# Weight splits moved from GpSimd to VectorE, and the last stage's weight conversion spread over more steps

## The chip, the cores and the metric

The kernel runs on one core of a Trainium2 chip. The metric is device time in microseconds for one execution, the median of three runs. The engines of the core are named as in the profile: PE is TensorE's matmul queue, PEld its weight loads, DVE is VectorE, ACT is ScalarE, POOL is GpSimd, SP is SyncE, which here issues most DMAs.

## The reference

The inputs are float32 except the last stage's two weights, which arrive as float64. Three stages follow one another on 2304 tokens of 512 values:

```
x   = local_attention(q, k, v) + upsampled(pooled_attention(q, k, v))   # 4 batches, 8 heads
e   = argmax(x @ w_gate + modality_bias[modality_id])                   # 8 experts
y   = prob[e] * (relu(x @ w1[e]) @ w2[e])                               # w1[e] 512x1024, w2[e] 1024x512
h   = y @ w_in                                                          # 512 -> 2048
out = (max(h, 0) + log1p(exp(-abs(h)))) @ w_out                         # 2048 -> 512
```

One pass of the array is less exact than the result is wanted. So every operand a of a matmul is kept as two float32r tensors, high = round(a) and low = a - high, and each product is three matmuls: high x high, low x high, high x low (lines L553, L556 and L557 of a helper).

## The kernel before, in words

**The attention and the gate** take the first 220 us or so. The gate computes the expert's logits of a group of tokens and turns them into a choice, a probability and a rank by some twenty small VectorE operations on tiles of 128 x 40 (L862 to L895 are the first), each of which needs the one before. For the last group, TensorE can go on only when these are done.

**The experts** work on slots of 128 rows. A slot gathers its rows (L522, an indirect DMA that GpSimd issues), multiplies by the expert's w1 (`gemm1`), applies relu (`h_t`), multiplies by w2 (`gemm2`), scales the result on ScalarE (L1171, `y`) and stores it. Two slots, 9 and 15, hold the remains of two experts each and are called mixed; 20 slots run for this input. Operands are split into high and low as well: `split_t` does so for the rows, with the subtraction on VectorE at L528 (`xl` for the input rows, `hl` for the hidden ones).

**The weights** come in parts of 128 x 1024 float32; a slot with an expert's weights of its own needs eight. A part is loaded to a buffer `raw`, and `split_part` makes of it `wh` (ScalarE copies and rounds, L332) and `wl` (raw minus wh, L333). Which engine does L333 is decided by the part's number i: for the first full slots' run (i < bounds[0]) GpSimd does it for every fourth part and for parts 4 to 7; for the last stage's parts c = 8 to 15 (i >= FF0 + CD) GpSimd does it always; VectorE does the others. That makes 45 of 152 splits on GpSimd. The subtraction needs `wh`, so it stands behind L332 of the same part.

**The conversion** turns the last stage's float64 weights into float32 by integer operations on halves of a part: SP loads a half (`conv_load`), and `conv_work` issues four operations, on ScalarE (L206, `cm`), VectorE (L209, `cy`, then L213) and GpSimd (L215, which adds `cm`). For the first eight parts (c < CD) this is done during the slots from 7 on as the code is written, and the result is stored to memory and loaded again like other weights. For parts 8 to 15 it is done within the last stage, straight into a `raw` buffer, and `split_part` follows.

**The last stage** has 18 tiles of 128 tokens in 6 groups of three, and 16 parts c of 128 hidden columns. A step is one group and one part: `ffn1` multiplies by the w_in part and applies the function with four or five VectorE operations (L1238, L1240, L1241, L1246; L1237 only from group 2 on), and two steps later `ffn2` multiplies by the w_out part. The list `steps` sets the order. Before, it goes (group 0, c 0 to 7), (group 1, c 0 to 7), (group 0, c 8 to 15), (group 1, c 8 to 15), then each later group with all 16 parts. `acts` hangs further work on the steps: the conversion of half i = 0 to 15 at step i + 2, the split of part 8 + i//2 in the same step as its second half, the gathers of a later group's rows (L1193, issued by GpSimd) and their transposes (`y_t`, with a small cast of an index column on VectorE, L1215, that needs the gather).

**What sets the order.** Each engine runs its own instruction queue in order, and an instruction that waits holds up all behind it. The order in a queue is chosen by a scheduler that simulates the program when it is built; instructions marked with `keep_in_program_order` keep the order in which they are written. So a change of one assignment can move other instructions too.

The choice of the engine for the subtraction, L332 to L334:

```
ins = (act.activation(out=hi, in_=r, func=ACTF.Copy),
       (pool if i >= FF0 + CD or (i % 4 == 3 or NR[0] <= i < PL) and i < bounds[0] else dve).tensor_tensor(
           out=lo, in0=r, in1=f32(hi), op=ALU.subtract))
```

Of the kernel before, what the change touches and what calls it, by code (L numbers as in the profile page):

```python
# [19 lines left out]
def tile_attention_moe_ffn(  # L20
# [30 lines left out]
    # Slots of 128 rows. A full one holds a block of one expert: the first NSTAT the first blocks of the expert with the most  # L51
    # rows before the last group, the others the further blocks of more than 64 rows. A mixed one (in MIX) holds two experts'
    # last 64 rows or fewer. Slots from SM on are for the draws that need them.
# [209 lines left out]
    def load_part(i):  # L263
        """Starts the load of a part, if the part before it in its tile is split."""
        kind, s, j = parts[i]
        at = raw_of(kind, s, j)
        if at not in raws or owner.get(at, i) not in split and at in owner:
            return False
        owner[at] = i
        t = raws[at]  # L270
        if kind == 3:
            x = sp.dma_start(out=t, in_=wf[s])
            if NR[0] <= s < 8:
                tc.keep_in_program_order(x)
        else:
            w = w1r if kind == 1 else w2r
            if s < NSTAT:
                if "star" not in eids:
                    eids["star"] = sp.value_load(star_i[0:1, 0:1], min_val=0, max_val=NE - 1)
                sp.dma_start(out=t, in_=w[bass.ds(eids["star"] * DM + j * 128, 128), :])  # L280
            else:
                if s not in eids:
                    eids[s] = sp.value_load(widx[0:1, dix[s]:dix[s] + 1], min_val=0, max_val=2 * NE - 1)
                e = eids[s]
                r = (e & (NE - 1)) * DM + j * 128
                if s >= SM:
                    sp.dma_start(out=t, in_=w[bass.ds(r, 128), :])
                else:
                    with tc.If(e < NE):
                        sp.dma_start(out=t, in_=w[bass.ds(r, 128), :])  # L290
        loaded.add(i)
        return True

    def ring_of(i):
        """0, 1: the two pools of the ring; 2: the further parts that the feed-forward holds."""
        if i < bounds[0]:
            return 0 if i % NRT < NR[0] else 1
        c = i - FF0
        return 0 if c < 0 or NRT - NR[0] <= c < NRT else 1 if c < NRT else 2

    def load_mixed(i):
        """The parts of two experts, not split."""
        kind, s, j = parts[i]
        at = ring_of(i)
        w = w1r if kind == 1 else w2r
        ts = []
        for a, nm in enumerate(("wh", "wl")):
            t = ring[at].tile([128, 1024], F32, tag=nm, name=nm, bufs=NR[at])
            d = NDF + 2 * MIX.index(s) + a
            if (s, a) not in eids:  # L310
                eids[s, a] = sp.value_load(widx[0:1, d:d + 1], min_val=0, max_val=NE - 1)
            sp.dma_start(out=t, in_=w[bass.ds(eids[s, a] * DM + j * 128, 128), :])
            ts.append(t)
        split[i] = ts

    def split_part(i):
        for n in range(i, min(i + 8, state["end"], FF0 + CD)):
            if parts[n][1] in MIX and parts[n][0] < 3:
                continue
            if n not in loaded and not load_part(n):  # L320
                break
        if parts[i][1] in MIX and parts[i][0] < 3:
            return load_mixed(i)
        at = ring_of(i)
        if at < 2:
            hi = ring[at].tile([128, 1024], F32R, tag="wh", name="wh", bufs=NR[at])
            lo = ring[at].tile([128, 1024], F32R, tag="wl", name="wl", bufs=NR[at])
        else:
            hi, lo = extra.pop(0)
        assert i in loaded or i >= FF0 + CD  # L330
        r = raws[raw_of(*parts[i])]
        ins = (act.activation(out=hi, in_=r, func=ACTF.Copy),  # L332
               (pool if i >= FF0 + CD or (i % 4 == 3 or NR[0] <= i < PL) and i < bounds[0] else dve).tensor_tensor(  # L333
                   out=lo, in0=r, in1=f32(hi), op=ALU.subtract))  # L334
        if PL <= i < PIN or i < NR[0]:
            tc.keep_in_program_order(ins[1])
            tc.keep_in_program_order(ins[0])
        if i >= FF0:
            for x in ins:
                tc.keep_in_program_order(x)  # L340
        split[i] = (hi, lo)

    def part(kind, s, j):
        """A part's two tensors; splits a few of those that follow, too."""
        i = where[kind, s, j]
        n = 2
        for k in range(i, min(i + state["ahead"] + 1, state["end"])):
            if k not in split and (k == i or n):
                split_part(k)
                n -= k > i  # L350
        return split[i]

    # ================= slot tables =================
# [7 lines left out]
    def slot_experts(bufs, pn):  # L361
        """Experts, columns of tokt and rows of the further full slots (0 to NDF) and of the halves of the mixed ones."""
# [17 lines left out]
        # full blocks of each expert, the further ones, and whether rows are left  # L380
# [24 lines left out]
        # the expert of each slot, plus NE where its weights are those of the full slot before or the slot is not used  # L405
# [8 lines left out]
        # the block within the expert, its column of tokt, its rows  # L414
# [16 lines left out]
        # whether the slots after each segment are used  # L431
# [5 lines left out]
    def runs():  # L437
        """Runs of full slots between mixed ones: first slot, count."""
# [10 lines left out]
    def tables(pl):  # L449
# [3 lines left out]
        # columns of tokt as rows  # L453
# [7 lines left out]
        # the rows of the further slots: columns of tokt, picked by a product with one-hot columns  # L461
# [13 lines left out]
        # compact order of the routed rows  # L475
# [110 lines left out]
    # ================= attention and routing =================  # L586
    def phase_a(actx):
# [12 lines left out]
        # Rows of a local tile: 64 queries of an even head, then of an odd head; columns: 64-query half, head pair, key.  # L600
# [21 lines left out]
        def pieces(t):  # L622
            """Runs of a tile's tokens within one batch: (row, count, batch, token of the batch)."""
# [74 lines left out]
        # Pooled attention. A product takes 48 queries of an even and an odd head (rows) and all keys (columns); a unit  # L698
        # is two such head pairs with all queries.
# [38 lines left out]
        def down_o(b, u):  # L738
            """64 rows for each head: the 48 of its queries, then (even) or before them (odd) 16 that don't count."""
# [21 lines left out]
        # local attention  # L761
# [75 lines left out]
        def gate_mm(t, ts):  # L837
            """Four products side by side, of 128 columns of x each (rows 32 k on, token), then their sum (token, expert)."""
# [12 lines left out]
        def gate(ts):  # L851
            """Three stages, each of which waits for the one before on another engine."""
# [13 lines left out]
            # the probability of the expert  # L866
# [3 lines left out]
            # the first of the largest  # L870
# [8 lines left out]
            # rank of each token among its expert's  # L879
# [32 lines left out]
            # place: row rr % 128 of block rr // 128  # L912
# [36 lines left out]
        def pick(pn):  # L949
            """The expert with the most rows so far (SR at most count; its later rows rank from SR on), and these rows."""  # L950
# [182 lines left out]
    # ================= experts and feed-forward =================  # L1133
    def phase_cd():
# [40 lines left out]
        # feed-forward  # L1175
# [5 lines left out]
        # Slots that hold the rows of the first groups for certain: of the further full slots 12 are used at least, with 65 rows  # L1181
        # or more, and with fewer than 128 in one for each expert at most.
# [38 lines left out]
        def ffn1(g, c):  # L1221
# [6 lines left out]
            # max(h, 0) + log1p(e), e = exp(-|h|), log1p(e) = ln(u) - ((u - 1) - e), u = 1 + e  # L1228
# [116 lines left out]
        steps = [(g, c) for c0 in (0, CD) for g in range(2) for c in range(c0, c0 + CD)]  # L1345
        steps += [(g, c) for g in range(2, len(groups)) for c in range(NFC)]
        acts = {i: [] for i in range(-1, len(steps))}
        for g in range(1, len(groups)):
            for j in range(GT):
                i0, i1 = (2 * j - 2, 2 * j + 1) if g == 1 else (steps.index((g - 1, 5 + 2 * j)), steps.index((g - 1, 11 + 2 * j)))  # L1350
                acts[max(i0, -1)].append(lambda t=groups[g][j]: gather_y(t))
                acts[i1].append(lambda g=g, j=j: y_t(g, j, acc(g) + j))
        conv_load()
        conv_load()
        for i in range(2 * CD):
            acts[i + 2].append(conv_work)
            acts[i + 2].append(conv_load)
            if i % 2:
                acts[i + 2].append(lambda c=CD + i // 2: split_part(FF0 + c))
# [4 lines left out]
        for i in range(len(steps) + LAG):  # L1364
            if i < len(steps):
                early_ = i < 2 * CD + 2
# [55 lines left out]
```

## Time and profile before

| | us |
|---|---|
| median of 3 runs | 960.98 (958.58 to 962.06) |
| span of the profiled execution | 959.4 (no device time of its own is given beside the span) |
| attention and gate | to about 220 |
| from there to slot 2's output | 220 to 266.3 |
| from slot 2's output to slot 7's output | 266.3 to 357.5 |
| slots 11 to 19 | 404.0 to 516 |
| last stage, groups 0 and 1 | 517 to 680.6 |
| last stage, group 2 | 680.6 to 748.7 |

The stages' ends are read from the timeline: a slot's output is its L1171 on ScalarE, the last stage's first matmul starts at 516.99, and the first output DMA of group 1 (which ends group 0 and 1's steps but for the last two) starts at 680.65, that of group 2 at 748.69.

How to read the rows below. In the table by stretch a row gives the stretch, its length, and for PE, PEld, DVE, ACT and POOL the busy time with the number of instructions; then the clock that TensorE was granted (1.00 is full), the share of the DMA engines that was busy and the GB/s moved. In a table of waits "PE p L557 <- DVE hl L528: 12.3, 3, 6.8" says that PE's matmuls of line 557 stood idle 12.3 us in total for VectorE's `hl` of line 528, three times, at most 6.8 us. A group by shape gives the count, the busy time, the mean duration in ns and the idle time of the engine just before such instructions with what ended it. In a timeline a row with x2 or more stands for so many instructions in succession.

### The profile page before, as it was taken

Reading aid. Unit: us, or ns where it says so; the run is one execution under the profiler, and the core shown is the slowest. Engines: PE = TensorE matmul, PEld = TensorE weight load, DVE = VectorE, ACT = ScalarE, POOL = GpSimd, SP = SyncE. Lnnn points to the kernel's source line nnn. Section 1 sums busy time; section 2 is a strip of 40 time slices with the busy share of each in tenths; the row PEclk is TensorE's granted clock in tenths of the full one; section 3 lists DMA queues with packets and bytes.
Section 4 is the critical chain, followed back from the end, with each engine's and each line's share of the span. In section 5 each row is a group of like instructions: output and inputs, shape, how many; then the busy total and the mean of one; then the engine's idle time right before and its main releaser. Section 6 shows DMA issues by size and latency. Waiting matters only on the chain. (4 is left out here: it accounts for less than half of the span.)

```text
span 959.4 us, 15330 instructions
## 1 busy us (share of the span) xinstructions
PE 870.1 (91%) x5356; PEld 738.0 (77%) x5356; DVE 663.3 (69%) x1226; ACT 549.2 (57%) x935; POOL 322.7 (34%) x308
## 2 busy tenths in 40 slices
PE   5788988969996789999999788999999999999996
PEld 4687887847775565686687687898999989989884
DVE  6486678685799994765764888855666666666662
ACT  3545554534877665776875666666554544555552
POOL 8324544453576764444330345502101100100001
PEclk9789899869998899999999989999999999999999
DMA  9999856545835578457553422101001000000000
GB/s 162 189 173 210 193 145 162 167 132 191 276 105 158 178 253 322 132 199 278 182 175 124 148 94 98 57 1 66 33 1 34 33 12 23 34 12 10 24 1 33
DMA packets 109111, 115.67 MB, mean 121 GB/s; under 512 B 68448, under 2 KB 83552, under 8 KB 109024
## 3 DMA queue, kind: packets, MB, share of 16 engines
q1 hardware_dynamic: 101072, 98.28, 35.9%
q0 software_dynamic: 4960, 16.28, 5.2%
q8 instruction: 44, 0.72, 0.3%
q10 hardware_dynamic: 2992, 0.04, 0.2%
q14 instruction: 43, 0.35, 0.1%
HBM read 92.93 MB, written 21.65 MB: 119 GB/s over the span
## 5 line engine op out<-in xcount | busy, mean ns | idle before, releaser
L332 ACT ACTIVATE wh<-raw 128x1024 fp32r<-128x1024 f32 x152 | 158.9, 1061 | 48.3 <-PE p L557 24.6
L333 DVE TENSOR_TENSOR wl<-raw,wh 128x1024 fp32r<-128x1024 f32 x107 | 153.3, 1460 | 26.1 <-ACT wh L332 23.3
L553 PE MATMUL p<-yh,wh 128*128 128x384 f32 x384 | 135.1, 352 | 15.1 <-DVE e L1240 14.0
L333 POOL TENSOR_TENSOR wl<-raw,wh 128x1024 fp32r<-128x1024 f32 x45 | 118.9, 2646 | 80.4 <-ACT wh L332 68.6
L556 PE MATMUL p<-yl,wh 128*128 128x384 f32 x384 | 132.3, 345 | 0.0
L557 PE MATMUL p<-yh,wl 128*128 128x384 f32 x384 | 132.2, 344 | 0.0
L553 PE MATMUL p<-wh,gh 128*128 128x512 f32 x288 | 113.8, 395 | 1.2 <-ACT gh L1245 1.1
L556 PE MATMUL p<-wl,gh 128*128 128x512 f32 x288 | 113.2, 393 | 0.0
L557 PE MATMUL p<-wh,gl 128*128 128x512 f32 x288 | 101.4, 395 | 0.0
L1239 ACT ACTIVATE u<-u 128x384 f32<-128x384 f32 x96 | 50.3, 524 | 85.4 <-DVE e L1238 85.1
L553 PEld LDWEIGHTS p<-yh,wh 128*128 128x128 f32 x384 | 74.5, 194 | 22.0 <-DVE e L1240 17.5
L1246 DVE TENSOR_TENSOR gl<-e,gh 128x384 fp32r<-128x384 f32 x96 | 56.2, 587 | 47.8 <-ACT gh L1245 47.1
L1245 ACT ACTIVATE gh<-e 128x384 fp32r<-128x384 f32 x96 | 50.3, 524 | 47.7 <-DVE e L1241 47.2
L556 PEld LDWEIGHTS p<-yl,wh 128*128 128x128 f32 x384 | 74.9, 195 | 3.1
L1193 POOL DMA_INDIRECT yg<-ys,pos x18 | 18.6, 1036 | 172.3 <-PE p L1210 159.1
L557 PEld LDWEIGHTS p<-yh,wl 128*128 128x128 f32 x384 | 74.5, 194 | 0.2
L1267 POOL DMA_INDIRECT out_dram<-o,ti x18 | 18.3, 1017 | 166.5 <-ACT o L1263 138.4
L1232 ACT ACTIVATE e<-p 128x384 f32<-128x384 f32 x96 | 46.8, 489 | 44.7 <-PE p L557 43.4
L557 PE MATMUL p<-wh,hl 128*128 128x512 f32 x144 | 58.9, 409 | 12.3 <-DVE hl L528 12.3
L1241 DVE TENSOR_TENSOR e<-e,u 128x384 f32<-128x384 f32 x96 | 62.5, 652 | 10.5 <-ACT u L1239 2.1
L1238 DVE SCALAR_TENSOR_TENSOR e<-u,e 128x384 f32<-128x384 f32 x96 | 58.5, 611 | 15.9 <-ACT u L1235 13.8
L557 PEld LDWEIGHTS p<-wh,gl 128*128 128x128 f32 x288 | 54.1, 188 | 12.8 <-DVE gl L1246 0.3
(257 smaller groups left out, 1916.1 us busy)
## 6 DMA issues: line engine op xcount, KB each, us to landing
raw<-in_moe_w_dram SPq DMA_DIRECT2D x40, 512.0 KB
cv<-in_moe_w_in_dram SPq DMA_DIRECT2D x16, 512.0 KB
cv<-in_moe_w_out_dram SPq DMA_DIRECT2D x16, 512.0 KB
wh<-in_moe_w_dram SPq DMA_DIRECT2D x16, 512.0 KB
wl<-in_moe_w_dram SPq DMA_DIRECT2D x16, 512.0 KB
vw<-in_v_dram SPq DMA_DIRECT2D x36, 144.0 KB
ys<-y SPq DMA_DIRECT2D x20, 256.5 KB
vg<-in_v_dram SPq DMA_DIRECT2D x16, 288.0 KB
```

What stands on the lines that cost most here:

```text
L332: ins = (act.activation(out=hi, in_=r, func=ACTF.Copy), (pool if i >= FF0 + CD or (i % 4 == 3 or NR[0] <= i < PL) and i < bounds[0] else d ...
L333: (pool if i >= FF0 + CD or (i % 4 == 3 or NR[0] <= i < PL) and i < bounds[0] else dve).tensor_tensor(out=lo, in0=r, in1=f32(hi), op=ALU.s ...
L553: i = pe.matmul(out=ps, lhsT=lh, rhs=rh, start=first, stop=False)
L556: pe.matmul(out=ps, lhsT=lh, rhs=rl, start=False, stop=False)
L557: pe.matmul(out=ps, lhsT=ll, rhs=rh, start=False, stop=last)
L1193: pool.indirect_dma_start(out=y, out_offset=None, in_=ys[0:rows], in_offset=bass.IndirectOffsetOnAxis(ap=pos[:, t:t + 1], axis=0))
L1232: act.activation(out=e, in_=ps, func=ACTF.Abs)
L1238: dve.scalar_tensor_tensor(out=e, in0=u, scalar=-1.0, in1=e, op0=ALU.add, op1=ALU.subtract)
L1239: act.activation(out=u, in_=u, func=ACTF.Ln)
L1241: dve.tensor_tensor(out=e, in0=e, in1=u, op=ALU.add)
L1245: act.activation(out=gh, in_=e, func=ACTF.Copy)
L1246: dve.tensor_tensor(out=gl, in0=e, in1=f32(gh), op=ALU.subtract)
```

## The change

L333 is always on VectorE. In the last stage, groups 0 and 1 still take parts 0 to 7 one group after the other; from part 8 on they take turns: (0,8), (1,8), (0,9), (1,9), (0,10), (1,10), then (0,11) to (0,15) and (1,11) to (1,15). The conversion of half i goes from step i + 2 (2 to 17) to step 4 + 6i//5 (4 to 22), and the split of a part from the step of its second half to the step after (6, 8, 11, 13, 15, 18, 20, 23). The transposes of group 2's rows go to steps 29, 30 and 31. `early_`, which puts a step's further work behind `ffn1` instead of ahead of it, holds for steps below 28 instead of 18. Comments are taken out, which shifts line numbers (by one from L334 on, so that L862 of before is L861).

```
-               (pool if i >= FF0 + CD or (i % 4 == 3 or NR[0] <= i < PL) and i < bounds[0] else dve).tensor_tensor(
-                   out=lo, in0=r, in1=f32(hi), op=ALU.subtract))
+               dve.tensor_tensor(out=lo, in0=r, in1=f32(hi), op=ALU.subtract))
...
-        steps = [(g, c) for c0 in (0, CD) for g in range(2) for c in range(c0, c0 + CD)]
+        steps = [(g, c) for g in range(2) for c in range(CD)]
+        for c in range(CD, NFC):
+            steps += [(0, c), (1, c)] if c < CD + 3 else [(0, c)]
+        steps += [(1, c) for c in range(CD + 3, NFC)]
...
+                if g == 2:
+                    i1 = 2 * NFC - GT + j
...
-            acts[i + 2].append(conv_work)
-            acts[i + 2].append(conv_load)
+            at = 4 + 6 * i // 5
+            acts[at].append(conv_work)
+            acts[at].append(conv_load)
             if i % 2:
-                acts[i + 2].append(lambda c=CD + i // 2: split_part(FF0 + c))
+                acts[at + 1].append(lambda c=CD + i // 2: split_part(FF0 + c))
...
-                early_ = i < 2 * CD + 2
+                early_ = i < 4 * CD - 4
```

VectorE's queue at the gate of the last group of tokens, before:

```order
L862 TENSOR_TENSOR lg<-b_2875,biast 128x40
L865 TENSOR_REDUCE gmx<-lg 128x5
L868 TENSOR_TENSOR ex<-lg,gmx 128x40
L872 TENSOR_TENSOR eq<-lg,gmx 128x40
L873 TENSOR_TENSOR eq<-eq,rev_73 128x40
L892 TENSOR_REDUCE gs<-ex 128x5
L875 TENSOR_REDUCE re<-eq 128x5
```

After:

```order
L333 TENSOR_TENSOR wl<-raw_3123,wh 128x1024
L333 TENSOR_TENSOR wl<-raw_3124,wh 128x1024
L861 TENSOR_TENSOR lg<-b_2875,biast 128x40
L333 TENSOR_TENSOR wl<-raw_3125,wh 128x1024
L864 TENSOR_REDUCE gmx<-lg 128x5
L333 TENSOR_TENSOR wl<-raw_3126,wh 128x1024
L867 TENSOR_TENSOR ex<-lg,gmx 128x40
L871 TENSOR_TENSOR eq<-lg,gmx 128x40
L872 TENSOR_TENSOR eq<-eq,rev_73 128x40
```

The subtractions of w2's first four parts, which were on GpSimd, now stand here: two ahead of the logits `lg`, one behind `lg` and one behind `gmx`.

VectorE's queue between the two halves of a slot's hidden rows and the input rows of a later one (`hl`, `xl`), in one of the slots 3 to 7, before:

```order
L528 TENSOR_TENSOR hl<-p_3933,hh 128x512
L209 TENSOR_SCALAR cy<-cv 128x512
L333 TENSOR_TENSOR wl<-raw_3123,wh 128x1024
L289 UNCONDITIONAL_BRANCH
L213 SCALAR_TENSOR_TENSOR cz<-cv,cy 128x512
L333 TENSOR_TENSOR wl<-raw_3124,wh 128x1024
L289 UNCONDITIONAL_BRANCH
L333 TENSOR_TENSOR wl<-raw_3125,wh 128x1024
L209 TENSOR_SCALAR cy<-cv 128x512
L289 UNCONDITIONAL_BRANCH x2
L1172 CAST y<-gidx 128x1
L528 TENSOR_TENSOR xl<-p_4004,xh 128x512
```

After, at the same tiles:

```order
L527 TENSOR_TENSOR hl<-p_3933,hh 128x512
L333 TENSOR_TENSOR wl<-raw_3123,wh 128x1024
L289 UNCONDITIONAL_BRANCH
L333 TENSOR_TENSOR wl<-raw_3124,wh 128x1024
L289 UNCONDITIONAL_BRANCH
L333 TENSOR_TENSOR wl<-raw_3125,wh 128x1024
L209 TENSOR_SCALAR cy<-cv 128x512
L289 UNCONDITIONAL_BRANCH
L333 TENSOR_TENSOR wl<-raw_3126,wh 128x1024
L527 TENSOR_TENSOR xl<-p_4004,xh 128x512
```

All four parts (`raw_3123` to `raw_3126`) are subtracted on VectorE, where there were three, and one operation of the conversion stands between them instead of three. Counted over whole slots, VectorE has 8 to 9 splits in each of the slots 3 to 7, where it had 6; the conversion, which is not changed in the code, is put later by the scheduler: 2 halves a slot in slots 4 to 7 and eight in slots 8 to 11, where there were 3 or 4 a slot in slots 4 to 7 and three in the two slots behind.

GpSimd's queue as the last stage begins (`yg` are gathered rows, `raw4` to `raw7` the buffers of the converted parts), before:

```order
L1193 DMA yg_7013<-ys_64,pos_92 128x513
L1193 DMA yg_7534<-ys_64,pos_92 128x513
L215 TENSOR_TENSOR raw4_86<-raw4_86,cm_7015 128x512
L215 TENSOR_TENSOR raw4_86<-raw4_86,cm_7074 128x512
L1193 DMA yg_7624<-ys_64,pos_92 128x513
L333 TENSOR_TENSOR wl_7083<-raw4_86,wh_7082 128x1024
L215 TENSOR_TENSOR raw5_87<-raw5_87,cm_7121 128x512
L215 TENSOR_TENSOR raw5_87<-raw5_87,cm_7173 128x512
L333 TENSOR_TENSOR wl_7182<-raw5_87,wh_7181 128x1024
```

After:

```order
L1192 DMA yg_7013<-ys_64,pos_92 128x513
L1192 DMA yg_7504<-ys_64,pos_92 128x513
L1192 DMA yg_7596<-ys_64,pos_92 128x513
L215 TENSOR_TENSOR raw4_86<-raw4_86,cm_7101 128x512
L215 TENSOR_TENSOR raw4_86<-raw4_86,cm_7153 128x512
L215 TENSOR_TENSOR raw5_87<-raw5_87,cm_7200 128x512
L215 TENSOR_TENSOR raw5_87<-raw5_87,cm_7243 128x512
L215 TENSOR_TENSOR raw6_88<-raw6_88,cm_7290 128x512
L215 TENSOR_TENSOR raw6_88<-raw6_88,cm_7368 128x512
```

The subtractions, one behind each second L215, are gone, and the two first gathers for group 2 (the second and third row, one of which stood behind two L215) stand ahead of the first L215. Ten more rows of L215 follow with nothing between.

## Rows read from the trace of the kernel before

**Rows 1.** Page, head.
```profile
span 959.4 us, 15330 instructions
```

**Rows 2.** Busy time by stretch, columns as said above.
```profile
200.00:220.00 20.00, 13.28 (x66) 9.51 (x64) 15.30 (x53) 6.93 (x13) 11.31 (x6) 0.61 0.24 86
220.00:266.30 46.30, 43.05 (x194) 35.10 (x195) 30.57 (x59) 31.70 (x41) 20.63 (x10) 0.93 0.71 245
266.30:357.50 91.20, 70.83 (x303) 56.03 (x302) 89.13 (x86) 60.41 (x82) 63.30 (x30) 0.91 0.52 171
400.00:500.00 100.00, 100.00 (x487) 75.74 (x486) 68.45 (x78) 77.03 (x100) 38.30 (x20) 1.00 0.55 194
517.00:680.60 163.60, 150.55 (x721) 134.91 (x722) 120.55 (x183) 104.33 (x203) 53.73 (x33) 0.95 0.24 81
680.60:748.70 68.10, 68.10 (x349) 61.60 (x348) 43.53 (x88) 34.78 (x69) 6.45 (x7) 1.00 0.07 24
```

**Rows 3.** Timeline, ScalarE: outputs of two slots in succession (start us, us, instruction).
```profile
404.00 0.69 ACT L1171 ACTIVATE y<-p,gw 128x512 f32<-128x512 f32 x1 [0.33 <-PE p L557]
...
416.55 0.69 ACT L1171 ACTIVATE y<-p,gw 128x512 f32<-128x512 f32 x1 [0.33 <-PE p L557]
```

**Rows 4.** Waits of PE, 266.3 to 357.5 us (sum, times, longest).
```profile
PE p L557 <- DVE hl L528: 12.3, 3, 6.8
```

**Rows 5.** Groups by shape, VectorE, 266.3 to 357.5 us (columns above).
```profile
L333 DVE TENSOR_TENSOR wl<-raw,wh 128x1024 fp32r<-128x1024 f32 x31 | 54.8, 1794 | 1.2 <-ACT wh L332 1.2
L209 DVE TENSOR_SCALAR cy<-cv 128x512 int32<-128x512 int32 x15 | 16.5, 1100 | 0.8 <-SPq L289 0.8
L213 DVE SCALAR_TENSOR_TENSOR cz<-cv,cy 128x512 int32<-128x512 int32 x14 | 13.3, 951 | 0.0
```

**Rows 6.** Groups by shape, GpSimd, 266.3 to 357.5 us.
```profile
L333 POOL TENSOR_TENSOR wl<-raw,wh 128x1024 fp32r<-128x1024 f32 x10 | 28.5, 2850 | 0.2 <-ACT wh L332 0.2
L215 POOL TENSOR_TENSOR cz<-cz,cm 128x512 int32<-128x512 int32 x14 | 23.1, 1650 | 16.7 <-issue 7.0 <-ACT wh L332 2.8 <-PE p L556 2.2
```

**Rows 7.** Duration of one line, whole program (min/median/max ns, first and last start).
```profile
L333 DVE TENSOR_TENSOR wl<-raw,wh x107: 1208/1219/6326, 166.5 to 543.6; 128x1024 fp32r<-128x1024 f32 x107
...
L333 POOL TENSOR_TENSOR wl<-raw,wh x45: 2343/2412/7082, 191.0 to 621.7; 128x1024 fp32r<-128x1024 f32 x45
...
L209 DVE TENSOR_SCALAR cy<-cv x32: 411/422/3005, 275.4 to 616.8; 128x512 int32<-128x512 int32 x32
...
L213 DVE SCALAR_TENSOR_TENSOR cz<-cv,cy x16: 675/680/2876, 277.3 to 367.1; 128x512 int32<-128x512 int32 x16
...
L215 POOL TENSOR_TENSOR cz<-cz,cm x16: 1264/1300/2253, 283.2 to 370.0; 128x512 int32<-128x512 int32 x16
```

**Rows 8.** Groups by shape, GpSimd, 400 to 500 us.
```profile
L333 POOL TENSOR_TENSOR wl<-raw,wh 128x1024 fp32r<-128x1024 f32 x13 | 31.4, 2417 | 33.3 <-ACT wh L332 21.6 <-DVE gw L547 7.1 <-PE p L1150 4.5
```

**Rows 9.** Timeline, GpSimd, at the gate.
```profile
201.02 9.31 POOL L333 TENSOR_TENSOR wl<-raw,wh 128x1024 fp32r<-128x1024 f32 x4 [2.40 <-ACT wh L332]
```

**Rows 10.** Timeline, VectorE, at the gate.
```profile
203.65 0.20 DVE L862 TENSOR_TENSOR lg<-b,biast 128x40 f32<-128x40 f32 x1 [3.53 <-PE b L849]
...
204.12 1.65 DVE L868 TENSOR_TENSOR ex<-lg,gmx 128x40 f32<-128x40 f32 x1
205.70 2.39 DVE L872 TENSOR_TENSOR eq<-lg,gmx 128x40 f32<-128x40 f32 x1
208.12 2.26 DVE L873 TENSOR_TENSOR eq<-eq,rev 128x40 f32<-128x40 f32 x1
```

**Rows 11.** Waits of PE, 517 to 680.6 us.
```profile
PE p L553 <- DVE e L1240: 13.0, 7, 3.8
```

**Rows 12.** Groups by shape, VectorE, 517 to 680.6 us.
```profile
L1241 DVE TENSOR_TENSOR e<-e,u 128x384 f32<-128x384 f32 x33 | 27.1, 826 | 3.2 <-ACT u L1239 1.2
...
L1240 DVE SCALAR_TENSOR_TENSOR e<-p,e 128x384 f32<-128x384 f32 x33 | 18.2, 553 | 0.7
```

**Rows 13.** Page, costliest groups: GpSimd's low halves.
```profile
L333 POOL TENSOR_TENSOR wl<-raw,wh 128x1024 fp32r<-128x1024 f32 x45 | 118.9, 2646 | 80.4 <-ACT wh L332 68.6
```

## The prediction

> **What bounds the kernel now.** I read the busy time by stretch first [rows 2]. The reader is to see two stretches in which PE, the engine that all stages share, is not full: 266.3 to 357.5 us, where VectorE is busy 89.13 of 91.20 us and PE 70.83, and 517 to 680.6 us, where PE is busy 150.55 of 163.60. From 400 to 500 us, and in the last stage's third group (680.6 to 748.7), PE is busy all the time at full clock: nothing is to be had there, and they give the floors. A slot takes 12.55 us when PE is never waited for (the two outputs of [rows 3]). Group 2's 16 steps take 68.1 us.
>
> Second, the waits of PE in the two stretches. In the first, PE is idle for 20.4 us (91.20 - 70.83), 12.3 of them in three waits for VectorE's low half of the hidden rows [rows 4], the other side of a full VectorE. In the second, 13.0 us, seven times, for VectorE's part of the softplus [rows 11].
>
> Third, why VectorE is full there. From 266.3 to 357.5 a split takes 1.794 us in the mean, L209 1.100 and L213 0.951 [rows 5]; the same instructions take 1.208, 0.411 and 0.675 us where nothing disturbs them [rows 7]. GpSimd in the same stretch does 10 splits and 14 L215 [rows 6]. So the excess on VectorE is 31 x 0.586 + 15 x 0.689 + 14 x 0.276 = 18.2 + 10.3 + 3.9 = 32.4 us. Undisturbed, GpSimd's own work would be 10 x 2.343 + 14 x 1.264 = 41.1 us [rows 7]. A microsecond of GpSimd's elementwise work thus costs VectorE 32.4/41.1 = 0.79 us. In the last stage L1241 shows the same: 826 ns against 553 ns for L1240, an instruction of that shape [rows 12].
>
> The Trainium skill, "SBUF — State Buffer", "Who interferes with whom", says more strictly that GpSimd shares VectorE's second port pair and that the pair is an exclusive lock for a whole instruction. By it the 0.79 would be 1.0; the 8 L215 left below would then cost VectorE 10.1 us and not 8.0, and the gain there would be 2 us less. I keep the row's 0.79.
>
> **The change part by part.** The sum is made against the profiled execution's span of 959.4 us [rows 1], 1.6 us under the median of 960.98; no device time of that execution stands beside its span, so I put differences onto the median.
>
> The engine of L333. A split moved takes 2.343 us from GpSimd, so 0.79 x 2.343 = 1.85 us of excess from VectorE, and adds 1.208 us to it: 0.64 us gained for each, where VectorE is last, and only where GpSimd's work did lie beside VectorE's.
>
> Gate. Four splits of GpSimd run from 201.02 to 210.33 [rows 9]; beside them three small VectorE operations on 128x40, of which `lg` shows the undisturbed 0.20 us, take 1.65, 2.39 and 2.26 us [rows 10]: 5.7 us lost. Afterwards two splits stand ahead of `lg`, in the 3.53 us that VectorE waits for PE anyway, and two behind it: 2 x 1.21 = 2.4 us on the path. Their `wh` must be ready, else the small operations queued behind them wait, and then PE; GpSimd's first waited 2.40 us for it, of which I charge half. Gain 5.7 - 2.4 - 1.2 = 2. Bounds: 5.7 gained, 2 lost (both waits in full).
>
> 220 to 266.3 us. PE is idle for 3.25 us of 46.30 in all, with the DMA engines 71% busy. I count nothing; bounds 0 and 3.
>
> Slots 3 to 7 (91.2 us). VectorE without the excess: 89.1 - 32.4 = 56.7. Ten more splits: +12.1. The order puts about six halves of the conversion to later slots: -6 x (0.41 + 0.68) = -6.5. GpSimd's 8 L215 left: 8 x 1.264 x 0.79 = +8.0. That is 70.3. VectorE is idle for 2.1 us now; with more instructions that wait in order I take 4: 74 us. PE's floor is 5 x 12.55 = 62.8, lower, so VectorE still decides, and the gain is 17. Given back later: 400 to 500 us has VectorE busy for 68.45 us and takes 13 more splits [rows 8], 15.7 us, to 84 of 100, so PE covers that; but the six halves (6.5 us, and 6 x 1.0 of collisions) and the splits of slots 8 to 10, where the first mixed slot's loads come too, fall between: I charge 4, a third of these 12.5. Net gain 13. If the cover is gone, the charge is all 12.5. Bounds: 0 and 28 (the floor, nothing given back).
>
> Last stage, groups 0 and 1 (163.6 us). Its floor is PE at full clock: 721 matmuls at the rate of 349 in 68.1 us are 140.7. The 22.9 us above it are the 13.0 us of waits and about 9.9 us of slower matmuls (150.55 busy against 140.7), the granted clock being 0.95 in this stretch and 1.00 in the next. VectorE is busy for 120.55 us now; eight splits more make 130.3 without any excess taken off, under 140.7. So the cause of the waits is not VectorE's sum, but bursts: conversions in sixteen successive steps, with GpSimd's L215 and splits beside them. The spread over 19 steps and the absent splits thin these, the 16 L215 remain. The turns of groups 0 and 1 move no work: each step needs the same matmuls. The split one step later has its `wh` ready. The two gathers ahead of the first L215 cost GpSimd about 1 us each, beside PE; group 2's transposes at steps 29 to 31 are issued once, as before, and `early_` only sets on which side of a step's products such work is written. SP's loads of the halves go with the steps. I leave a third of the 22.9 us, for the L215 and for a cast of a gathered column that still stands early in VectorE's queue: 148.3 us, gain 15.3. Bounds: 5 and 21.
>
> Sum: 2 + 13 + 15.3 = 30.3 us, so 930.7, say 931.
>
> **The rivals.** A: the forecast, 931, from 922 to 942.
>
> B: the slots give nothing net. Ten more splits and the in-order waits keep VectorE last, and what is saved in slots 3 to 7 comes back in slots 8 to 11. For it: VectorE is 98% busy there, and every microsecond of estimate errs on its queue. Against: 32.4 us of excess is too much to vanish. 961 - 2 - 15.3 = 944.
>
> C: all stretches reach PE's floor: 961 - 4 - 28 - 21 = 908. For it: 400 to 500 us shows that slots at 12.55 us are possible. Against: the 70 us of VectorE work that I count in slots 3 to 7.
>
> D, slower: the waits that GpSimd took are carried by VectorE's queue. GpSimd's low halves stood idle 80.4 us, 68.6 of them for ScalarE's `wh` [rows 13]. Put into VectorE's order, such a wait holds up the operands' low halves and the softplus behind it, and PE after these. VectorE's slack is about 16 us per 100 from 400 us on, 18 up to the last stage, and 140.7 - 130.3 = 10 in that. All 68.6 us carried would be 68.6 - 28 = 41 us against the gain of 30: 972. It decides from about 58 us carried. For it: [rows 8] shows 33.3 us of such idle time in 100 us. Against: in these rows GpSimd came early and waited because it had nothing else; the scheduler puts VectorE's split where its `wh` is due, and VectorE's own 31 splits wait 1.2 us [rows 5].
>
> E: the one left behind is GpSimd. With splits in rows of four on VectorE (4 x 1.21 = 4.8 us), an L215 beside them is held up, the split behind it gets its part late, and VectorE waits in order. The rows have L215 at 1.650 us in the mean against 1.264 [rows 6, 7], so a little of this is there now. In the last stage each of eight splits would wait for a step's four operations and a split, 4 x 0.55 + 1.21 = 3.4 us, so 27 us onto 140.7: 168, 4 us worse than now; with the gate's 2 and the slots' 13 that is 950.
> The Trainium skill (same page, "SBUF: two separate sides") speaks for E: whichever of the two starts first has the pair for its whole instruction, "the other fully blocks". By it, an L215 would wait out at most the VectorE instruction before it, 1.21 us, if the turns alternate, and the trace's 0.39 us of excess for an L215 lies under that.
>
> **How the numbers follow.** A 0.5, B 0.2, C 0.11, D 0.08, E 0.11. The predicted time is A's. The range of 8 in 10 takes all of A and B, most of E, and the near part of C: 915 to 953. What a measurement of this kernel can tell from no change is about 0.5%, 4.8 us: under 956 is faster, over 966 slower. A, C and nearly all of B and E are faster: 0.84. Within 0.5%: 0.09, from the tails of B and E and a little of D. Slower: 0.07, the greater part of D.
>
> **What would show it.** Right: splits on VectorE at 1.21 to 1.4 us in slots 3 to 7, and L209 near 0.6 us; these slots at about 15 us each and VectorE still nearly full; PE's wait for L1240 under 5 us in the last stage, its granted clock near 1.00 there, and 148 us for groups 0 and 1; the gate's `ex` and `eq` at 0.2 us. B shows as slots 8 to 11 longer than before by what slots 3 to 7 gained. D shows as idle time of VectorE before L333 released by `wh`, tens of microseconds, with PE waits on `hl` from 400 us on, where there are none now. E shows as L215 over 2.5 us in the mean. The forecast is wrong if the excess per GpSimd microsecond is not what made VectorE slow (then the splits stay near 1.8 us with GpSimd idle beside them), or if the last stage's waits come from the gathers or the operations' order, and stay at 13 us.

## The result, and the profile after

The changed kernel takes 923.25 us in the median of four runs (918.01 to 926.1) against 961.52 us for the kernel before in the same comparison: a ratio of 0.9606, with a 95% interval of 0.9557 to 0.9654. The span of the profiled execution is 923.4 us, 36.0 us under the 959.4 of [rows 1]. The forecast was 931, so the gain was 8 us larger than the sum.

The busy time by stretch, cut at the same events as in [rows 2] (gate; slot 2's output to slot 7's; 100 us of later slots; groups 0 and 1 of the last stage; group 2), with the columns explained there:

```profile
200.00:220.00 20.00, 11.61 (x63) 8.11 (x62) 14.66 (x61) 7.03 (x13) 2.00 (x2) 0.83 0.35 107
265.15:332.20 67.05, 63.31 (x293) 50.49 (x292) 67.05 (x83) 56.27 (x76) 24.23 (x14) 1.00 0.56 186
377.40:477.40 100.00, 97.96 (x466) 73.61 (x465) 78.75 (x94) 75.10 (x99) 15.88 (x9) 0.98 0.60 204
491.70:644.40 152.70, 143.39 (x720) 127.35 (x721) 111.58 (x191) 103.04 (x203) 32.49 (x26) 1.00 0.28 87
644.40:712.60 68.20, 68.20 (x349) 61.68 (x348) 43.70 (x88) 34.72 (x70) 6.40 (x6) 1.00 0.07 24
```

From slot 2's to slot 7's output it is 67.05 us and was 91.20; VectorE is still busy all of it, and PE 63.31. Groups 0 and 1 take 152.70 us and took 163.60. TensorE's granted clock is 1.00 in both, where it was 0.91 and 0.95. Group 2 is the same within 0.2 us. By the events themselves (outputs, first matmul, first output DMA), in us, with the runs that are told of below:

| | gate and slots 0 to 2, to | slots 3 to 7 | slots 8 to 19 | groups 0 and 1 |
|---|---|---|---|---|
| before | 266.3 | 91.2 | 159.5 | 163.6 |
| after | 265.1 | 67.0 | 159.6 | 152.6 |
| e1, engine only, old steps | 262.3 | 67.0 | 160.0 | 150.9 |
| e2, order only | 268.9 | 89.6 | 159.5 | 160.0 |
| e3, last stage's splits on GpSimd | 262.9 | 67.0 | 161.3 | 161.0 |
| e4, parts 4 to 7 on GpSimd | 271.2 | 72.4 | 164.5 | 150.6 |
| e5, scratch subtractions | 265.8 | 100.7 | 162.7 | 151.0 |
| e6, scratch memsets | 264.0 | 67.2 | 157.4 | 152.6 |
| e7, no L215 on GpSimd | 265.9 | 65.2 | 162.0 | 149.0 |

The first column moves by some us from run to run of one kernel: the changed kernel run again (e10) has 262.1, 67.0, 161.0 and 154.5. So 1 to 3 us in it, or 2 us in the last column, prove nothing.

VectorE's groups by shape in slots 3 to 7, which answer to [rows 5], then GpSimd's to [rows 6], and PE's wait for `xl`, after and, below it, before:

```profile
L333 DVE TENSOR_TENSOR wl<-raw,wh 128x1024 fp32r<-128x1024 f32 x40 | 50.7, 1304 | 0.0
L213 DVE SCALAR_TENSOR_TENSOR cz<-cv,cy 128x512 int32<-128x512 int32 x8 | 6.8, 854 | 0.0
...
L209 DVE TENSOR_SCALAR cy<-cv 128x512 int32<-128x512 int32 x8 | 3.3, 415 | 0.0
```

```profile
L215 POOL TENSOR_TENSOR cz<-cz,cm 128x512 int32<-128x512 int32 x8 | 14.9, 1860 | 32.3 <-ACT wh L332 15.6 <-DVE y L1171 15.3 <-DVE cz L213 0.7
```

```profile
PE p L556 <- DVE xl L527: 2.1, 2, 1.5
```

```profile
PE p L557 <- DVE xl L528: 8.1, 4, 2.8
```

There are 40 splits instead of 31, and together they take 50.7 us instead of 54.8: 1.304 us each and not 1.794. L209 is down from 1.100 to 0.415 us. What is left of collisions is now mostly GpSimd's: its L215 takes 1.860 us. PE's wait for `hl`, 12.3 us [rows 4], is gone, and of 8.1 us for `xl` 2.1 are left.

The gate on VectorE, which answers to [rows 10]; below it ScalarE's copy of the first of the four parts, and PE's waits from 200 to 220 us:

```profile
207.54 0.19 DVE L861 TENSOR_TENSOR lg<-b,biast 128x40 f32<-128x40 f32 x1
207.65 1.21 DVE L333 TENSOR_TENSOR wl<-raw,wh 128x1024 fp32r<-128x1024 f32 x1
208.78 0.19 DVE L864 TENSOR_REDUCE gmx<-lg 128x5 f32<-128x40 f32 x1
208.88 1.21 DVE L333 TENSOR_TENSOR wl<-raw,wh 128x1024 fp32r<-128x1024 f32 x1
210.02 0.19 DVE L867 TENSOR_TENSOR ex<-lg,gmx 128x40 f32<-128x40 f32 x1
210.13 0.19 DVE L871 TENSOR_TENSOR eq<-lg,gmx 128x40 f32<-128x40 f32 x1
```

```profile
203.71 1.06 ACT L332 ACTIVATE wh<-raw 128x1024 fp32r<-128x1024 f32 x1 [5.41 <-DMA raw<-in_moe_w_dram]
```

```profile
PE b L845 <- ACT xT L834: 4.9, 1, 4.9
PE b L888 <- DVE cacc L882: 1.6, 1, 1.6
```

The small operations take 0.19 us, as undisturbed ones do, and the two splits between them cost 2.4 us. But before that ScalarE waited 5.41 us for the part's load, with the gate's `xT` queued behind the copy, and PE 4.9 us for `xT`. In before PE waited 5.0 us a little later, for the slow small operations; the products behind that start at 211.57 us now and started at 211.37.

In the last stage PE's wait, which answers to [rows 11], VectorE's groups for [rows 12], and two pairs of timeline rows: what VectorE waited for, and PE behind it:

```profile
PE p L552 <- DVE e L1239: 9.1, 7, 1.7
```

```profile
L1240 DVE TENSOR_TENSOR e<-e,u 128x384 f32<-128x384 f32 x33 | 20.0, 615 | 1.7 <-ACT u L1238 0.4
L1239 DVE SCALAR_TENSOR_TENSOR e<-p,e 128x384 f32<-128x384 f32 x33 | 18.0, 552 | 0.6
L333 DVE TENSOR_TENSOR wl<-raw,wh 128x1024 fp32r<-128x1024 f32 x12 | 14.6, 1220 | 7.2 <-ACT wh L332 7.2
```

```profile
511.15 0.15 DVE L1214 CAST ti<-yg 128x1 int32<-128x1 f32 x1 [3.40 <-DMA yg<-ys,pos]
...
581.12 1.23 DVE L333 TENSOR_TENSOR wl<-raw,wh 128x1024 fp32r<-128x1024 f32 x1 [3.14 <-ACT wh L332]
```

```profile
512.43 0.44 PE L552 MATMUL p<-yh,wh 128*128 128x384 f32 x1 [1.49 <-DVE e L1239]
...
584.74 0.44 PE L552 MATMUL p<-yh,wh 128*128 128x384 f32 x1 [1.72 <-DVE e L1239]
```

L1240 (L1241 of before) is down from 826 to 615 ns, beside an unchanged 552 for the operation with an operand in PSUM. PE still waits seven times, 9.1 us. Behind the wait at 512.43 stands a cast that waits 3.40 us for a gathered column (of group 1's rows: by the code, the gathers that now stand ahead of the first L215 are group 1's, and not group 2's as the section on the change has it); behind that at 584.74 a split that waits 3.14 us for ScalarE's copy, in order, with the softplus behind it. VectorE's splits wait 7.2 us for `wh` in this stretch. Over the whole program, VectorE's splits (before, then after) are

```profile
L333 DVE TENSOR_TENSOR wl<-raw,wh 128x1024 fp32r<-128x1024 f32 x107 | 153.3, 1460 | 26.1 <-ACT wh L332 23.3
```

```profile
L333 DVE TENSOR_TENSOR wl<-raw,wh 128x1024 fp32r<-128x1024 f32 x152 | 187.6, 1256 | 34.8 <-ACT wh L332 31.8
```

### The profile page after: what moved, and what is told of

The parts are those of the page before. It is cut to its first block, busy times and chain, and to the rows that moved or that the text cites. A ratio compares the mean times of both kernels' runs of the same rounds, so it can differ in the third digit from the quotient of the medians.

```text
span 923.4 us, 15325 instructions
## 1 busy us (share of the span) xinstructions
PE 853.3 (92%) x5356; PEld 725.9 (79%) x5356; DVE 654.7 (71%) x1271; ACT 547.1 (59%) x935; POOL 214.8 (23%) x263
## 5 line engine op out<-in xcount | busy, mean ns | idle before, releaser
L333 DVE TENSOR_TENSOR wl<-raw,wh 128x1024 fp32r<-128x1024 f32 x152 | 187.6, 1256 | 34.8 <-ACT wh L332 31.8
L552 PE MATMUL p<-yh,wh 128*128 128x384 f32 x384 | 131.6, 343 | 11.3 <-DVE e L1239 10.1
L556 PE MATMUL p<-yh,wl 128*128 128x384 f32 x384 | 129.4, 337 | 0.0
L555 PE MATMUL p<-yl,wh 128*128 128x384 f32 x384 | 129.3, 337 | 0.0
L555 PEld LDWEIGHTS p<-yl,wh 128*128 128x128 f32 x384 | 72.2, 188 | 3.0
L1237 DVE SCALAR_TENSOR_TENSOR e<-u,e 128x384 f32<-128x384 f32 x96 | 55.2, 577 | 13.4 <-ACT u L1234 11.2
L552 PEld LDWEIGHTS p<-wh,gh 128*128 128x128 f32 x288 | 54.1, 188 | 10.5 <-ACT gh L1244 1.5
L1240 DVE TENSOR_TENSOR e<-e,u 128x384 f32<-128x384 f32 x96 | 55.3, 579 | 9.0 <-ACT u L1238 1.3
L555 PEld LDWEIGHTS p<-wl,gh 128*128 128x128 f32 x288 | 54.2, 188 | 8.7
L552 PE MATMUL p<-wh,hh 128*128 128x512 f32 x144 | 58.9, 409 | 1.8 <-ACT y L1170 1.5
```

Of the source, the lines that this page charges most:

```text
L333: dve.tensor_tensor(out=lo, in0=r, in1=f32(hi), op=ALU.subtract))
L552: i = pe.matmul(out=ps, lhsT=lh, rhs=rh, start=first, stop=False)
L555: pe.matmul(out=ps, lhsT=lh, rhs=rl, start=False, stop=False)
L556: pe.matmul(out=ps, lhsT=ll, rhs=rh, start=False, stop=last)
L1237: dve.scalar_tensor_tensor(out=e, in0=u, scalar=-1.0, in1=e, op0=ALU.add, op1=ALU.subtract)
L1240: dve.tensor_tensor(out=e, in0=e, in1=u, op=ALU.add)
```

## The experiments

**Engine or order.** Three runs take the change apart. e1 puts L333 on VectorE in the kernel before and changes nothing else; e2 is the changed kernel with the old choice of engines; e3 gives back only the last stage's eight splits:

```
e1   kernel before:  dve.tensor_tensor(out=lo, in0=r, in1=f32(hi), op=ALU.subtract)
e2   changed kernel: (pool if i >= FF0 + CD or (i % 4 == 3 or NR[0] <= i < PL) and i < bounds[0] else dve).tensor_tensor(...)
e3   changed kernel: (pool if i >= FF0 + CD else dve).tensor_tensor(...)
```

Expected of e1: 

> Only L333 is moved to VectorE; steps, conversion and split steps as before. Theory of the collisions (GpSimd's elementwise work slows VectorE): slots 3 to 7 take 67 us as in the changed kernel instead of 91, and groups 0 and 1 of the last stage some 157 us, about half of the way from 163.6 to 152.6, since 8 of 24 GpSimd instructions are gone there: 961 - 24 - 7 = 930. Rival (the order and the spread make the last stage's gain): slots 67 us, last stage still 163 us: 936.

Expected of e2: 

> The changed kernel with L333 on the engines of before, so only the turns, the spread and the later transposes. Collisions: slots 3 to 7 stay at 91 us, last stage's groups 0 and 1 at about 158: 955. Rival (order and spread): 91 us and 152.6 us: 950. If most of the last stage's gain is neither's alone: 163 us, no change.

Expected of e3: 

> The changed kernel, but the last stage's eight splits of parts 8 to 15 are on GpSimd again. Collisions: 8 x 2.34 us of GpSimd beside VectorE cost 5 us in the last stage, 158 for groups 0 and 1: 928. Rival (a split in VectorE's queue, which waits there for ScalarE's copy, is what leaves PE's three waits of 1.7 us): these waits go and the stage takes 148 us or so: 919.

e1: 920.55 us, ratio 0.9586 (0.9545 to 0.9627). e2: 961.13 us, 1.0005 (0.9982 to 1.0027). e3: 931.65 us, 0.9685 (0.9650 to 0.9719). The engine alone gives the whole gain, and the turns, the spread and the later transposes give the whole program nothing that can be measured. For e2 that is the time of the last of the three cases, though its last stage is shorter than the 163 us said there. Its stretches by the same view (slots 3 to 7, groups 0 and 1):

```profile
268.90:358.50 89.60, 70.48 (x302) 55.48 (x302) 87.62 (x85) 60.29 (x81) 62.27 (x30) 0.90 0.53 173
518.00:678.00 160.00, 145.54 (x720) 128.78 (x721) 115.53 (x183) 102.84 (x203) 54.88 (x33) 0.99 0.26 83
```

Groups 0 and 1 take 160.0 us, 3.6 less than before, and start 1.0 us later; the execution profiled, 958.73 us, is the fastest of e2's ten, and their median shows none of this. With the splits on VectorE the new order is not better than the old: 152.6 and, run again, 154.5 us against 150.9 in e1. In e1 VectorE's splits of this stretch wait 0.9 us for `wh`, not 7.2:

```profile
L333 DVE TENSOR_TENSOR wl<-raw,wh 128x1024 fp32r<-128x1024 f32 x12 | 16.4, 1369 | 0.9 <-ACT wh L332 0.9
```

e3 is 8.4 us slower than the changed kernel, all of it in the last stage. That is 1.05 us for each split given back, and PE's waits there are

```profile
PE p L553 <- DVE e L1240: 13.3, 11, 3.0
```

so the rival, that a split waiting in VectorE's queue costs more than GpSimd's company, falls.

**Gate.** e4 gives back parts 4 to 7 alone:

```
(pool if NR[0] <= i < PL else dve).tensor_tensor(
```

Expected of e4: 

> The changed kernel, but parts 4 to 7 (the four splits at the gate) are on GpSimd again. As predicted for the gate: 2 us slower, 925. From the trace after, where the gate's last matmul starts at the same time as before (211.6 against 211.4 us): no difference within 0.3%, with the small operations at 1.6 to 2.4 us again.

940.28 us, 0.9771 (0.9725 to 0.9817): 17 us over the changed kernel's median, which neither theory had, and 14.4 in the spans of the profiles. The gate is as in before; its rows on VectorE (the addition to `tokt`, which ends the group of tokens ahead, and the small operations):

```profile
205.08 0.29 DVE L936 TENSOR_TENSOR tokt<-tokt,b 128x144 f32<-128x144 f32 x1
...
211.48 1.92 DVE L868 TENSOR_TENSOR ex<-lg,gmx 128x40 f32<-128x40 f32 x1
213.32 2.38 DVE L872 TENSOR_TENSOR eq<-lg,gmx 128x40 f32<-128x40 f32 x1
```

From that `tokt` to slot 0's output it is 38.8 us, 34.9 in the changed kernel (35.7 in e10), and 36.7 in the kernel before (236.5 - 199.8). So some 4 us of the 14.4 are the gate's. Another 10 are in slots 3 to 19, where the splits are where they were, but the scheduler has put conversions and loads in another order; 5 are won back in slots 1 and 2 and in the last stage. And 5 us are lost before 200 us, in the attention, whose instructions stand in the same order; the profile shows a granted clock of 0.74 from 128 to 148 us there, where the changed kernel's shows 1.00. The cause of these 5 us is open.

**Company.** The changed kernel with work on GpSimd beside VectorE's that nobody waits for, on a scratch tile (cut to the lines that matter):

```
+        if dmy and i % 4 == 3 and i < bounds[0]:      # e12: i % 8 == 3
+            for _ in range(2):
+                pool.tensor_tensor(out=dmy[0], in0=dmy[0], in1=dmy[0], op=ALU.subtract)   # e6: pool.memset(dmy[0], 0.0)
...
+        dmy.append(... .tile([128, 512], F32, name="dm"))
```

Expected of e5: 

> The changed kernel with 66 subtractions of 128x512 more on GpSimd during the slots, on a scratch tile that nothing else touches (it adds work and changes nothing computed), in the number that the old splits would have in those slots. Nobody waits for them. Collisions: each costs GpSimd 1.27 us and VectorE 0.4 to 0.8 of that where it is full; some 25 to 40 of them beside the full slots 2 to 7 make these 12 to 35 us longer, total 935 to 955. Rival (what the change took away was the wait of others for GpSimd's results and its order, not the company): no difference over 3 us, 923.

Expected of e6: 

> As the run before, but the 66 additions are memsets of 128x512, which read nothing. If only GpSimd work that reads this memory holds VectorE up: 923, L333 at 1.21 to 1.3 us as in the changed kernel. If any GpSimd access does: longer, half or more of what the subtractions cost.

Expected of e12: 

> As e5 with 32 scratch subtractions instead of 66. If the price is per microsecond of GpSimd's work beside a full VectorE: about half of e5's 38 us, 940 to 943. If it is a threshold (VectorE has slack for some): under 930; if mere presence does it: near 960.

e5: 961.21 us, 1.0017 (0.9988 to 1.0046): the time of before, with all splits on VectorE. e12: 943.24 us, 0.9823 (0.9780 to 0.9865). e6: 920.57 us, 0.9605 (0.9542 to 0.9667), as the changed kernel. VectorE's groups of slots 3 to 7 in e5 (lines are one later there, so L334 is the split, L210 and L214 the conversion), and the scratch operations over the whole program:

```profile
L334 DVE TENSOR_TENSOR wl<-raw,wh 128x1024 fp32r<-128x1024 f32 x43 | 74.4, 1769 | 0.0
L214 DVE SCALAR_TENSOR_TENSOR cz<-cv,cy 128x512 int32<-128x512 int32 x7 | 9.9, 1412 | 0.0
L210 DVE TENSOR_SCALAR cy<-cv 128x512 int32<-128x512 int32 x8 | 9.1, 1145 | 0.4 <-SPq L290 0.4
```

```profile
L337 POOL TENSOR_TENSOR dm<-dm x66: 1037/1900/2075, 217.0 to 376.4; 128x512 f32<-128x512 f32 x66
```

The split takes 1.769 us and L210 1.145, much as in [rows 5], and L214 1.412, more than there. Nothing waits for `dm`, and neither VectorE nor PE waits for GpSimd anywhere in this stretch, so this is company and no dependency. A stretch of the timeline at its plainest (GpSimd, then VectorE, then PE):

```profile
265.81 16.37 POOL L337 TENSOR_TENSOR dm<-dm 128x512 f32<-128x512 f32 x9
...
270.18 6.01 DVE L334 TENSOR_TENSOR wl<-raw,wh 128x1024 fp32r<-128x1024 f32 x3
...
283.24 1.21 DVE L334 TENSOR_TENSOR wl<-raw,wh 128x1024 fp32r<-128x1024 f32 x1
...
276.85 1.22 PE L560 MATMUL p<-wh,xl 128*128 128x512 f32 x2 [9.26 <-DVE xl L531]
```

Nine subtractions in succession take 1.82 us each, where the shortest takes 1.04. Beside them three splits take 2.00 us each; as soon as GpSimd pauses one takes 1.21. Each of the two engines is slowed while the other works. The row of PE is what it costs: `xl` stands behind these three splits and three more just ahead of them, and PE waits 9.26 us for it. The memsets, which read nothing, leave the durations where they were:

```profile
L334 DVE TENSOR_TENSOR wl<-raw,wh 128x1024 fp32r<-128x1024 f32 x40 | 50.7, 1302 | 0.0
...
L210 DVE TENSOR_SCALAR cy<-cv 128x512 int32<-128x512 int32 x8 | 3.4, 426 | 0.0
```

```profile
L337 POOL MEMSET dm<- x66: 524/526/686, 218.9 to 278.6; 128x512 f32 x66
```

They are all done by 279 us, so they lie beside only the first part of slots 3 to 7, and e12 is the run to hold them against: its 32 subtractions stand at the same place (217.3 to 288.6) and take GpSimd about as long when undisturbed (33 us; the memsets 35). VectorE's splits beside the memsets (266.2 to 279.1 us) and, below, beside e12's subtractions (266 to 288.6 us):

```profile
L334 DVE TENSOR_TENSOR wl<-raw,wh 128x1024 fp32r<-128x1024 f32 x9 | 10.6, 1216 | 0.0
```

```profile
L334 DVE TENSOR_TENSOR wl<-raw,wh 128x1024 fp32r<-128x1024 f32 x11 | 20.3, 1888 | 0.0
```

The Trainium skill ("SBUF — State Buffer", "Who interferes with whom") has the rule: a VectorE operation with two inputs from SBUF and a GpSimd operation that reads it contend for a shared port pair, by an exclusive lock. The traces agree with it in the kind, e6 against e12 above all; in the size, by estimate, a split and a subtraction that alternated in full would take 1.21 + 1.04 = 2.25 us, and the row has 2.00.

Twice the subtractions cost 38.0 us (e5 over the 923.25) and half of them 20.0 (e12): 0.58 and 0.62 us for each, near to proportional.

**No elementwise work on GpSimd from the slots on.** e7 is e1 with L215 on VectorE as a bitwise or, for which ScalarE's scale in L206 is 6% lower; e11 is e7 again with more rounds. The rounding of the lowest bit differs, as the text on record says.

```
...
-            pool.tensor_tensor(out=z, in0=z, in1=m, op=ALU.add)
+            dve.tensor_tensor(out=z, in0=z, in1=m, op=ALU.bitwise_or)
```

Expected of e7: 

> L333 on VectorE with the old steps (as in e1), and L215 on VectorE too, as a bitwise or (the lowest bit of a weight is rounded a little otherwise; ScalarE's scale is 6% lower for it). So GpSimd has no elementwise work from the slots on. Collisions: L209 at 0.42 us and L1238, L1241 at 0.56 us in the last stage; VectorE gains 32 operations of about 0.7 us and loses what L215 costs it, 16 x 1.27 x 0.4 to 0.8 in each half: no change in the slots, 0 to 6 us faster in the last stage: 914 to 920. Rival (VectorE's own operations are the bound and L215 is cheap): 5 to 10 us slower in the slots, 925 to 930.

Expected of e10: 

> The changed kernel unchanged, beside e9 and e11 on one chip: 921 to 924.

Expected of e11: 

> e7 unchanged, with more rounds: if L215's absence is worth what the last stage's durations say, 2 to 4 us under the changed kernel; if not, the same within 0.3%.

e7: 918.87 us, 0.9562 (0.9497 to 0.9627); e11: 916.41 us, 0.9559 (0.9525 to 0.9592), beside e10, the changed kernel again, with 921.74 us, 0.9604 (0.9572 to 0.9635). It is some 5 us faster, though the two intervals still overlap. The last stage's operations are at their undisturbed durations:

```profile
L1240 DVE TENSOR_TENSOR e<-e,u 128x384 f32<-128x384 f32 x33 | 18.3, 554 | 2.4 <-ACT u L1238 1.0
L1239 DVE SCALAR_TENSOR_TENSOR e<-p,e 128x384 f32<-128x384 f32 x33 | 18.3, 553 | 0.6
...
L209 DVE TENSOR_SCALAR cy<-cv 128x512 int32<-128x512 int32 x16 | 6.7, 420 | 1.4 <-DMA cv<-in_moe_w_in_dram 1.4
```

**Transposes and the gate's order.** e8 is e1 with group 1's transposes at steps 3, 5 and 7; e9 is e7 with the splits of parts 4 to 7 held behind the gate:

```
e8   (2 * j - 2, 2 * j + 3) if g == 1 else ...
e9   if i < PIN:                  # was: if PL <= i < PIN or i < NR[0]
```

Expected of e8: 

> L333 on VectorE with the old steps (as in e1), and group 1's rows are transposed at steps 3, 5, 7 instead of 1, 3, 5. If the wait of PE for 2.87 us near 511 us in e1 comes from VectorE's cast that waits for a gathered column: it goes, 3 us faster, 917. Rival (the next burst takes its place): no difference, 920.

Expected of e9: 

> As e7 (no elementwise work on GpSimd from the slots on), and the copies and subtractions of parts 4 to 7 are held in the written order, which puts them behind the gate's last small operations. If ScalarE's queue, where a copy that waits for its weight stands ahead of the gate's xT, is what costs PE 4.9 us at the gate after the change: that wait and the 1.6 us behind it go, 4 to 6 us at the gate less what slot 0 waits for its w2, total 913 to 916. Rival (slot 0 then waits for the splits): no difference to e7, 919 to 921.

e8: 920.12 us, 0.9593 (0.9539 to 0.9647), no difference to e1: the one long wait is gone, smaller ones stand at other places. e9: 915.68 us, 0.9536 (0.9506 to 0.9567), the lowest of all, but the same as e11. At the gate PE's waits for `xT` and for the small operations are gone (from `tokt` to the next `tokt` 9.8 us instead of the 15.6 of e11), and slot 0 pays for it (from there to its output 25.9 us instead of 17.3). Two of ScalarE's copies wait 5.31 and 1.46 us for their loads there, slot 0's output `y` is queued behind them, and PE waits for it:

```profile
PE p L552 <- ACT y L1170: 4.8, 1, 4.8
```

## Why the prediction was right, and where its steps were not

The main step held: GpSimd's elementwise work was what made VectorE slow in the slots, and taking the splits from it gained more than nine more splits cost. e5 and e12 show it with the cause alone added, and e6 with GpSimd busy at the same place but not reading. That the total lies within A's range, 1 us above its lower end, is in part luck: the slots gave 11 us more than the sum had, the last stage 4 and the gate 1 less. Against the spans, the sum of 30.3 us became 36.0 like this.

- **Slots 3 to 7: 17 forecast, 24.1 measured.** VectorE stayed the bound, as said, at 67 instead of 74 us. Two terms were mis-sized. The eight L215 left cost VectorE not 8.0 us but, by the same reckoning (mean over shortest duration), 40 x 0.096 + 8 x 0.179 = 5.3. And the 4 us charged for waits in order did not come: VectorE is busy 67.05 of 67.05 us. These are 6.7 of the 7.1 us; that nine splits came over and not ten makes another 1.2, and about 1 us the other way is not accounted for. D's argument, that GpSimd's idle time [rows 13] would be carried over, was wrong: over the whole program VectorE's splits wait 31.8 us for `wh` and waited 23.3, so of GpSimd's 68.6 us 8.5 came over. PE's waits for `hl` from slot 8 on, D's sign, are 2.0 us.
- **Given back later: 4 forecast, 0 measured**: from slot 7's output to the last stage it is 159.5 us before and 159.6 after. The charge itself did come, 4.9 us in slots 9 to 12 by their outputs, but slot 8, for which the sum had nothing, is 4.1 us shorter (14.5 and 18.6 us). Slots 8 to 11 together are as long as before, so B falls.
- **Last stage: 15.3 forecast, 11.0 measured.** The step that failed is the one on the bursts: the spread and the turns add nothing once the engine is changed (e1 has the shorter stage without them, and e2 gains nothing in all, though its stage is 3.6 us shorter in the one trace), and the engine, which the sum counted only as a part of it, is enough by itself (e1: 163.6 to 150.9 us; e3 gives 8.4 back). What was left was set at a third, 7.6 us; it is 12: 9.1 us of waits for VectorE, where under 5 were said, and 2.7 of slower matmuls (PE busy 143.39 us against 140.7). "The split one step later has its `wh` ready" was wrong: 7.2 us of waits, which e1 does not have. This is D's mechanism in small, and it was not in the sum.
- **Gate: 2 forecast, 1.1 to slot 2's output, which is within what moves from run to run, and none at the gate itself.** The small operations did recover to 0.2 us. But the 1.2 us charged for `wh` was not the wait that counted: ScalarE's in-order copy behind a load is, and PE's 4.9 us for `xT` replaced the 5.0 us. The splits on GpSimd are behind by 1.8 us in the kernel before and by 3.9 in e4, to slot 0's output; e9 shows that moving the splits away shifts the wait to slot 0. What bounds this place, as far as these runs go, is loads of weights with ScalarE's copies waiting for them in order.
- **E** asked for L215 over 2.5 us. GpSimd is indeed the side that waits more now, 1.860 us, but neither PE, VectorE nor ScalarE waits for it in the slots, and in the last stage L215 has a median of 1.381 us.

C's floor was not reached: slots 3 to 7 would take 62.8 us at it, and e7 has 65.2.

## What to carry to other kernels

When GpSimd shares elementwise work with a VectorE that is full, reckon what its company costs: here it was 0.52 (the eight L215 left: 5.3 us for 10.1) to 0.79 [rows 5 to 7] of GpSimd's own undisturbed time, and 0.56 in the time of the kernel (e5: 0.58 us for 1.04). By these, an estimate for a subtraction of 2.34 us on GpSimd is 1.2 to 1.9 us, and VectorE does it itself in 1.21. Look for it as one shape with two durations (1.2 and 1.8 us), and as a short operation beside a long one of the other engine; test it by adding scratch work that nobody waits for. And when an edit goes with an engine change, run each alone: the reordering, most of the diff, was worth nothing that the medians show.

## What was not expected of the hardware

L209 has a single tensor as input and is still slowed by GpSimd's subtractions (0.42 us against a mean of 1.1), while L1239 and L527, whose first input is in PSUM, are not (552 and 680 ns, before and after). The Trainium skill ("VectorE: DVE Perf Modes", "Mode 2×_2P — use both read ports for one tensor") says that an operation with one tensor and a constant may use both read ports; its 0.41 us for 512 elements, under 0.68 for L213 of the same size, agrees, though no run here looks at the ports themselves.
